# Where the held last product goes at two joins between matmul groups

## Chip, cores and metric

One core of one Trainium2 chip. The metric is the device time of one execution in microseconds (us). The kernel before took 721.73 us (median of 3 runs, 721.68 to 721.85).

## The reference

Layer norm of `x` (2048 tokens of 1024), then two branches on the normed `xn`: a dilated local attention and a gated MLP, joined at the end.

```python
x = A_x
xn = _layernorm(x, axis=-1)
s = _A_ref(xn, A_wqkv, A_wo)                 # qkv = xn @ wqkv; attention over 8 keys, 2 apart; @ wo
g = _silu(_B_ref(xn, B_w1, B_w3, B_w2))      # (silu(xn @ w1) * (xn @ w3)) @ w2
return x + s * g
```

## The kernel before: what the change touches

The q/k/v products and the MLP's first layer run in groups of seven matmul products (a Strassen-like scheme that saves the eighth). A product is eight matmuls of 128x128 weights against 512 columns. A group has three accumulators in PSUM: `pa` ("a" in the profile: aq, am), `pe` ("e") and `pb` ("b"). ScalarE copies a into b, so that b goes on from a's first product.

```python
def seven(key, A, B, e11, e12, e22, e21, snap=None):
    ...
    if snap is None:
        pa = bank2(f"a{key}")
        for i in I:
            mm(pa[:, i], a11[i], b11, True)          # product 1, into a
    pe = bank2(f"e{key}")
    for i in I:
        mm(pe[:, i], s1[i], t1, True)                # product 2, into e
    pb = bank2(f"b{key}")
    act_copy(pb[:], pa[:] if snap is None else snap) # ScalarE: a -> b
    sp5 = k4(f"p{key}")
    act_copy(sp5[:], pe[:])
    if snap is None:
        for i in I:
            mm(pa[:, i], a12[i], b21, False)         # product 3, onto a: has to follow a -> b
        e11(pa)
        flush()                                      # the held product of the group before
    for i in I:
        mm(pb[:, i], s2[i], t2, False)               # product 4, onto b
    su2 = k4(f"u{key}")
    act_copy(su2[:], pb[:])                          # ScalarE: copy of b
    flush()
    ...                                              # products 5 (e12) and 6 (e22: VectorE reads b)
    def tail():
        for i in I:
            mm(pb[:, i], a22[i], t4, False)          # product 7, onto b
        e21(pb)                                      # ScalarE: copies the result out
    pend.append(tail)                                # held for the next group

def qkv_copy(t, c, j0):
    def f(ps, *a):
        ...
            if a:
                ...                                  # VectorE adds
            else:
                nc.scalar.copy(out=d, in_=ps[:])     # e11 and e21 of a q/k/v group
    ...

    qkv_seven(1, 1, wk0, wk1, sk, step)              # k, second half
    flush()                                          # first join
    with behind("v"):
        qkv_sums(wq0, wq1, sk, True)
    qkv_seven(2, 1, *wv, sv, step)                   # v, second half
    qkv_seven(0, 1, wq0, wq1, sk, step)              # q, second half
    flush()                                          # second join, then the MLP
```

So product 7 of a group normally runs after product 3 of the next one. At the two joins `flush()` forced it out at once. (`behind(key)` makes an instruction issue after the one last recorded under that key.)

## Time and profile before

| | before |
|---|---|
| device time, median of 3 | 721.73 us |
| span of the profiled run | 720.1 us |
| PE busy | 712.5 us, 99% |
| granted clock | 0.998 |
| gap between products at the first join | 0.28 us |
| gap at the second join | 0.24 us |

The gaps are not a row of the profile. I measure them from the start times of products in the timeline: the start of a product, less the start of the product before it, less 0.216 us for each of that one's matmuls. The shown end of a matmul won't do, as the prediction explains. The lines of the profile before stand in the prediction.

### The profile page before, as it was taken

To read this page: it belongs to the slowest core of one execution; us is meant where nothing else is said; L and a number is where in the kernel's file an instruction comes from. 1 tells how busy PE (TensorE), PEld (TensorE's weight loads), DVE (VectorE), ACT (ScalarE), POOL (GpSimd) and SP (SyncE) were. 2 spreads that over 40 slices of the span, in tenths; PEclk is the share of its full clock that TensorE was granted. 3 is DMA by queue.
4 is the path that set the end of the run, shared out by engine and by line. 5 is a ranking of instruction groups with operands and counts; after the bars stand their busy time and mean duration, and the time that the engine had idled before them with its cause. 6 is when DMAs were issued, how large, how long until landed. Compare 5 with 4: busy or idle time off the path is not lost.

```text
span 720.1 us, 8820 instructions
## 1 busy us (share of the span) xinstructions
PE 712.5 (99%) x3367; PEld 346.2 (48%) x3367; DVE 625.6 (87%) x697; ACT 314.1 (44%) x329; POOL 95.7 (13%) x162
## 2 busy tenths in 40 slices
PE   8999999999999999999999999999999999999997
PEld 6655565654444444444444444444444444444443
DVE  7996879779879878978999999969859989998975
ACT  5745334356545456555545311024464563120234
POOL 1011100012300000233111000000435004000001
PEclk9999999999999999999999999999999999999999
DMA  9956257867754523457756647469799444463616
GB/s 333 267 146 176 82 185 228 274 228 242 240 174 160 178 85 117 153 205 264 251 169 216 203 132 240 155 189 385 172 279 348 127 152 138 156 205 130 194 55 117
DMA packets 119242, 139.52 MB, mean 194 GB/s; under 512 B 17696, under 2 KB 94496, under 8 KB 118560
## 3 DMA queue, kind: packets, MB, share of 16 engines
q1 hardware_dynamic: 104656, 97.01, 43.3%
q0 software_dynamic: 14544, 41.95, 17.9%
q8 instruction: 26, 0.43, 0.3%
q14 instruction: 16, 0.13, 0.1%
HBM read 96.21 MB, written 38.80 MB: 187 GB/s over the span
## 4 chain that ended last, share of the span: by engine, by line
PE 93%; DVE 2%; ACT 1%; DMA 1%; issue 1%; SPq 0%; DVEq 0%; ACTq 0%
PE bm L151 20%; PE am L151 13%; PE em L151 13%; PE bq L151 9%; PE db L151 8%; PE da L151 7%; PE de L151 6%; PE eq L151 6%; PE aq L151 3%; PE wb L151 3%; PE af L151 2%; PE wa L151 1%; PE we L151 1%; PE af L1038 1%; DMA wring<-in_A_wqkv_dram 1%
## 5 line engine op out<-in xcount | busy, mean ns | idle before, releaser
L151 PEld LDWEIGHTS <-wring 128*128 128x128 f16 (+1 forms) x1792 | 183.4, 103 | 204.2 <-issue 1.6
L151 PEld LDWEIGHTS <-h_sb 128*128 128x128 f16 (+1 forms) x1056 | 109.6, 104 | 118.1 <-issue 0.4
L151 PE MATMUL bm<-xs,wring 128*128 128x512 f16 x504 | 117.4, 379 | 0.1
L151 PE MATMUL am<-xT,wring 128*128 128x512 bf16 x336 | 79.7, 379 | 0.1
L151 PE MATMUL db<-wring,h_sb 128*128 128x512 f16 x336 | 73.2, 379 | 0.0
L481 DVE TENSOR_TENSOR BC<-Ep,vT 128x2048 bf16<-128x2048 bf16 x56 | 66.6, 1216 | 0.1
L426 DVE TENSOR_TENSOR pt<-qt,kT 128x4096 bf16<-128x4096 bf16 x24 | 54.9, 2289 | 0.6
L664 DVE TENSOR_TENSOR um<-em,um 128x1024 f32<-128x1024 f32 x28 | 34.2, 1222 | 21.1 <-PE em L151 20.3
L666 ACT ACTIVATE g<-um 128x1024 bf16<-128x1024 f32 x28 | 29.6, 1057 | 48.6 <-DVE um L664 48.6
L151 PE MATMUL da<-wring,h_sb 128*128 128x512 bf16 x224 | 49.0, 379 | 0.0
L467 POOL DMA_DIRECT2D Ep<-pb x64 | 38.0, 601 | 54.0 <-DVE pb L463 48.3
L151 PE MATMUL bm<-h_sb,wring 128*128 128x512 f16 x168 | 39.7, 379 | 0.0
L151 PE MATMUL em<-xT,wring 128*128 128x512 bf16 x168 | 39.7, 379 | 0.0
L151 PE MATMUL em<-xs,wring 128*128 128x512 f16 x168 | 39.7, 379 | 0.0
L161 ACT COPY bm<-am 128x1024 f32<-128x1024 f32 x28 | 27.9, 998 | 26.0 <-PE am L151 26.0
L491 DVE TENSOR_TENSOR oT<-oT,BC 128x2048 bf16<-128x2048 bf16 x32 | 39.0, 1218 | 0.3
L161 ACT COPY pm<-em 128x1024 f32<-128x1024 f32 x28 | 28.4, 1013 | 20.0 <-PE em L151 20.0
L161 ACT COPY um<-bm 128x1024 f32<-128x1024 f32 x28 | 28.4, 1013 | 18.9 <-PE bm L151 18.9
L685 ACT CAST g<-bm 128x1024 bf16<-128x1024 f32 x28 | 28.3, 1010 | 17.4 <-PE bm L151 17.4
L679 DVE TENSOR_TENSOR h_sb<-bm,pm 128x1024 bf16<-128x1024 f32 x21 | 25.6, 1217 | 5.1 <-PE bm L151 5.0
L428 DVE TENSOR_TENSOR pt<-pt 128x2048 bf16<-128x2048 bf16 x24 | 29.3, 1221 | 0.4
L489 DVE TENSOR_TENSOR BC<-BC 128x2048 bf16<-128x2048 bf16 x24 | 29.3, 1220 | 0.4
(191 smaller groups left out, 996.4 us busy)
## 6 DMA issues: line engine op xcount, KB each, us to landing
wring<-in_B_w_dram SPq DMA_DIRECT2D x61, 512.0 KB, 4.4
wring<-t_dram SPq DMA_DIRECT2D x16, 512.0 KB, 3.9
t_dram<-wring POOLq DMA_DIRECT2D x14, 512.0 KB, 3.9
wring<-t_dram SPq DMA_DIRECT2D x16, 384.0 KB, 5.0
wring<-in_B_w_dram SPq DMA_DIRECT2D x12, 384.0 KB, 4.8
wring<-in_A_x_dram SPq DMA_DIRECT2D x16, 256.0 KB, 4.7
Ep<-pb POOLq DMA_DIRECT2D x64, 64.0 KB, 4.7
wring<-in_A_wo_dram SPq DMA_DIRECT2D x8, 512.0 KB, 5.7
```

The source lines that it names most:

```text
L151: anchor["pe"] = nc.tensor.matmul(ps, lhsT=lhs[k], rhs=rhs[k], start=(first and k == 0), stop=(k == n - 1), skip_group_check=not first,)
L161: nc.scalar.copy(out=out_, in_=in_)
L426: nc.vector.tensor_mul(p_t[:], q[:], kT[:, :, o:o + CH])
L428: nc.vector.tensor_add(p_t[:, 0:4, :], p_t[:, 0:4, :], p_t[:, 4:8, :])
L467: nc.gpsimd.dma_start(out=pr[c][r:P:NR, :, sq * P:(sq + 1) * P], in_=pb[sq * 32:(sq + 1) * 32, :, :])
L481: nc.vector.tensor_mul(dst, E[:, w, :].unsqueeze(1).to_broadcast([P, n, CH]), vT[:, js, o:o + CH])
L489: nc.vector.tensor_add(B, B, C)
L491: nc.vector.tensor_add(A, A, B if w0 else C)
L664: v = nc.vector.tensor_add(su2[:], pe[:], su2[:])
L666: nc.scalar.activation(out=hl["g"][:, :, CH:], in_=su2[:], func=ACTF.Silu)
L679: anchor["v"] = nc.vector.tensor_add(h[:, :, CH:], pb[:], sp5[:])
L685: nc.scalar.copy(out=hl["g"][:, :, 0:CH], in_=pb[:])
```

## The change

Its intent is to let the held product at the two joins wait as it does everywhere else, so that ScalarE makes the new group's copy of a into b first.

```diff
     def act_copy(out_, in_):
         with hp():
-            nc.scalar.copy(out=out_, in_=in_)
+            return nc.scalar.copy(out=out_, in_=in_)
@@ seven
-        act_copy(pb[:], pa[:] if snap is None else snap)
+        anchor["pb"] = act_copy(pb[:], pa[:] if snap is None else snap)
@@ qkv_copy
-                    nc.scalar.copy(out=d, in_=ps[:])
+                    with behind("pb"):
+                        nc.scalar.copy(out=d, in_=ps[:])
@@ the calls
     qkv_seven(1, 1, wk0, wk1, sk, step)
-    flush()
     with behind("v"):
         qkv_sums(wq0, wq1, sk, True)
     qkv_seven(2, 1, *wv, sv, step)
     qkv_seven(0, 1, wq0, wq1, sk, step)
-    flush()
```

## The prediction

> **What bounds the kernel now.** I read the first part of the page first (busy time by engine), then the busy times of five stretches, then the chain of waits near each of the two joins, and last the timeline, instruction by instruction, around the joins and in a later group that the change doesn't touch.
>
> The page's span and busy times:
>
> ```profile
> span 720.1 us, 8820 instructions
> PE 712.5 (99%) x3367; PEld 346.2 (48%) x3367; DVE 625.6 (87%) x697; ACT 314.1 (44%) x329; POOL 95.7 (13%) x162
> ```
>
> The matmul engine (PE) is busy for 99% of the span. The change neither adds nor removes a matmul, so it can gain only what PE loses in gaps. In the view of busy times by stretch the two joins lie in the first and third of these (us of the stretch, its length, then PE):
>
> ```profile
> 102.00:118.00 16.00, 15.88 (x75) 9.48 (x73) 13.82 (x16) 5.95 (x6) 0.53 (x1) 1.00 0.72 237
> 118.00:145.00 27.00, 27.00 (x127) 16.36 (x126) 23.24 (x28) 10.90 (x11) 1.60 (x3) 1.00 0.74 249
> 145.00:172.00 27.00, 26.93 (x131) 13.63 (x129) 22.38 (x32) 17.86 (x19) 1.99 (x3) 1.00 0.79 252
> ```
>
> A stretch without a join shows no idle PE; those with one show 0.12 and 0.07 us. The granted clock is 1.00 in all three. These small figures understate the loss, as the timeline shows. First, what a steady group looks like (timeline, later):
>
> ```profile
> 191.55 1.89 PE L151 MATMUL am<-h_sb,wring 128*128 128x512 bf16 x8
> ...
> 193.28 1.89 PE L151 MATMUL em<-h_sb,wring 128*128 128x512 f16 x8
> ...
> 193.48 1.00 ACT L161 COPY bm<-am 128x1024 f32<-128x1024 f32 x1 [1.07 <-PE am L151]
> ...
> 195.01 1.89 PE L151 MATMUL am<-h_sb,wring 128*128 128x512 bf16 x8
> ```
>
> A product of eight matmuls starts every 1.73 us, 0.216 us per matmul. The third product adds onto the accumulator "a", so it has to follow the copy of "a" into "b" on ScalarE (ACT). That copy starts 0.20 us after the next product has begun (the last "a" matmul still has to land), ends at 194.48, and the third product starts at 195.01 on its own pace: 0.53 us to spare. Now the chain of waits at the first join:
>
> ```profile
> 105.90 1.51 PE aq L151 x7
> 107.41 1.74 PE bq L151 x8
> 109.15 0.03 ACTq L367
> 109.18 0.04 issue
> 109.22 1.01 ACT pk L367
> 110.23 0.92 ACT bq L161
> 111.15 0.04 issue
> 111.20 1.89 PE aq L151 x8
> ```
>
> The chain leaves PE here for two copies on ACT in a row. The last product of the old group (bq at 107.41) ends, its result is copied out (pk, 1.01 us), only then is the new group's "a" copied (bq<-aq), and then PE goes on. The timeline at the second join has the same pattern:
>
> ```profile
> 156.57 1.89 PE L151 MATMUL bq<-h_sb,wring 128*128 128x512 f16 x8
> ...
> 158.30 0.38 PE L151 MATMUL am<-xT,wring 128*128 128x512 bf16 x1
> ...
> 158.50 1.01 ACT L367 CAST h_sb<-bq 128x1024 bf16<-128x1024 f32 x1 [4.09 <-PE bq L151]
> 158.51 1.89 PE L151 MATMUL em<-xs,wring 128*128 128x512 f16 x8
> ...
> 159.41 1.02 ACT L161 COPY bm<-am 128x1024 f32<-128x1024 f32 x1
> ...
> 160.48 1.89 PE L151 MATMUL am<-xT,wring 128*128 128x512 bf16 x8
> ```
>
> **What the Trainium skill says.** (1) Its page "PSUM — Partial Sum Buffer", section "Engine vs sequencer instructions", says that the queues of ScalarE and VectorE are strict FIFO and that matmuls start and complete in program order. The trace agrees: at 158.50 the old group's cast runs, and the new group's copy, whose data were complete by about 158.7 (0.20 us after e began at 158.51), starts at 159.41. (2) The same page, section "PSUM bank collisions raise a hardware error", says that a bank has to be guarded by semaphores against a second engine. That is why the third product waits for the copy of "a" even though it only adds to it; the wait shows as 111.15 to 111.20. (3) "TensorE: Matmul & The Clock Gate", section "Back-to-back issue gap", gives N/2.4 + 2.5 ns, 216 ns at N=512, for one isolated gap, and about 131 ns sustained. The trace has 0.216 us per matmul in a sustained stream, so here the first figure holds and the second doesn't. (4) "Perfetto Trace Analysis", section "Tensor Engine Instruction (MATMUL, LD_WEIGHTS)", says that the profile's end of a matmul is an estimate. The trace bears that out: one matmul is shown as 0.379 us but they start 0.216 us apart, so 0.16 us of every PE gap is covered by the modelled end. I therefore measure gaps from starts.
>
> **The change, part by part.** It removes two calls that force out the held last product at the joins k to v (near 107 us) and q to the MLP (near 157 us). The held product then goes where it goes in all other groups: after the new group's first three products. It also ties the two plain copies of a q/k/v group behind the latest "a" to "b" copy, so that ACT takes that one first. I built the changed program and compared the order of its instructions with that of the kernel before, engine by engine.
>
> PE, first join: before a(7), old tail(8), a(1), e(8), a(8), then b; after a(8), e(8), a(8), old tail(8), then b. Same 32 matmuls, 32 times 0.216 = 6.91 us. Before, the first starts at 105.74 (timeline) and the b product at 112.92: 7.18 us. The stall is thus visible: e starts at 109.19, so the next product could start at 109.19 + 1.73 = 110.92, and it starts at 111.20. That is 0.28 us. (Less the 0.16 that the modelled end covers, it is the 0.12 of the first stretch.)
>
> PE, second join: after a(8), old tail(3), e(8), a(8), old tail(5), then b; the tail is split in two but has the same eight matmuls. Before, e at 158.51 + 1.73 = 160.24 against a start at 160.48: 0.24 us (less 0.16 is the 0.07 of the third stretch).
>
> Is each wait of the new order met in time? Times are on the old clock. First join: a from 105.74, e 107.47, third product 109.19. The copy of "a" starts at 107.47 + 0.20 = 107.67 and takes 1.02: 108.69, so 0.50 us to spare. The tail comes at 110.92 and needs VectorE's read of the same accumulator, which was done at 107.17. The old product's copy then runs from about 112.9 to 113.9, and the next copy that PE needs (of b, before 114.89 in the old trace, 0.28 sooner now) is still free to start on time. Second join: a at 155.06, three tail matmuls at 156.79 (VectorE reads that accumulator 155.26 to 156.48, so 0.3 to spare), e at 157.44, third product at 159.16, with the copy of "a" done by 156.79 + 0.20 + 1.02 = 158.01. Tail at 160.89, b at 161.97 against 162.20 before. ACT then has silu of "a" (1.02 us) from about 161.1, the old cast about 162.2 to 163.2, and the copy of b can start at 163.9: no queue.
>
> VectorE and GpSimd keep their order. On the sync engine's queue two small swaps follow: at the first join the store of v goes ahead of that of k; at the second one 512 KB weight load moves ahead of two copies of x to the output and one spill. That load went out at 165.24 before because it waits for a store; its data are first read by VectorE at 179.14, nearly 14 us later, so this isn't on the path.
>
> Sum: 0.28 + 0.24 = 0.52 us off PE's stream, nothing added on the path. 721.73 - 0.52 = 721.21, some 0.07%.
>
> **Rivals.** First, the gain is given back later. Measured by starts, PE after 20 us has only two more stalls above 0.1 us: 0.28 at 287.45 (ACT: table load, exponential, two copies) and 0.22 at 505.01 (a chain from a weight load through VectorE and ACT). If either were timed by something that doesn't move with PE, it would swallow the gain and the time would stay at 721.7. Against it: both chains start from PE in the view of the chain (the silu of "am" at 282.19; the load issued at 482.97 straight after PE work), so they should slide. VectorE at 87% is the engine that could lag: in 156 to 177 it runs without a break, so the second join's 0.24 isn't passed to it at once. The exponential at 167.01 waits for it, and the next "a" copy at 170.34 queues behind that; PE needs that copy at 172.13 - 0.52 = 171.61, and it would end at about 171.06. Tight, but met; later VectorE idles again (1.25 us at 190.09) and catches up.
>
> Second, the copies collide at the new place: the held product's cast delays the copy of b, and PE waits at the fourth product instead. That would take back up to 0.3 us per join, 721.4 to 721.7. Against it: in all groups without a forced flush this order already runs with no gap.
>
> Third, the moved transfers: three transfers of 512 KB pile up after 165 us rather than at 160, beside loads for the next groups. If one landed over 8 us late, VectorE's sums and then PE would wait, and the time would rise by a microsecond or more. The slack of 14 us against a landing of about 4 us speaks against it.
>
> Fourth, PE's stall at the joins is not really ACT's order, and the gap persists: 721.7. The chain's two adjacent copies with no idle time between speak against it.
>
> **Range and chances.** The three runs before lie within 0.17 us. Full gain is 721.2; half given back 721.5; a slightly better fit of the other stalls and another chip's scatter may reach 720.8. I take 720.8 to 721.65. Two per cent is 14 us; nothing of that size is in reach: faster 0.01, same 0.98, slower 0.01.
>
> **What would show it.** In the profile after, the pieces of ACT should be gone from the chain at 109 to 111 and 158 to 160 us; starts of products should be 1.73 us apart through both joins; busy PE in the first stretch should be 16.00 of 16.00; the copy of "a" should come before the old cast on ACT; the stalls near 287 and 505 should be there still, at 0.2 to 0.3 us, about 0.5 us earlier. The prediction is wrong if a new PE gap stands in the 20 us after either join, if the gaps near 287 or 505 grow by what was gained, or if the weight load of 512 KB holds up VectorE near 179 us.

## The result, and the profile after

The changed kernel took 721.31 us (median of 6 runs, 721.21 to 721.43), beside 721.91 us for the kernel before (6 runs, 721.68 to 722.16). The ratio is 0.9992, with a 95% interval of 0.9979 to 1.0005. A ratio is the mean time of one kernel's fast runs over that of the other's of the same rounds, so not quite the ratio of these medians. The interval reaches past 1, so by itself it doesn't prove a gain of this size. What speaks for it is that every run of the changed kernel was below every run of the kernel before, and the trace.

The page of the changed kernel, its span and busy times:

```profile
span 719.5 us, 8821 instructions
PE 713.1 (99%) x3367; PEld 346.4 (48%) x3367; DVE 625.7 (87%) x697; ACT 314.4 (44%) x329; POOL 96.0 (13%) x162
```

The matmuls are the same 3367. Busy times by stretch (first and third of the stretches shown before; after the stretch and its length stand the busy us of PE, its weight loads PEld, VectorE DVE, ScalarE ACT and GpSimd POOL, then the granted clock and the DMA engines' share and GB/s):

```profile
102.00:118.00 16.00, 16.00 (x76) 9.69 (x75) 13.82 (x17) 6.07 (x6) 0.53 (x1) 1.00 0.70 234
145.00:172.00 27.00, 27.00 (x132) 13.57 (x130) 22.38 (x33) 18.04 (x18) 1.99 (x3) 1.00 0.70 221
```

PE no longer idles in either. The chain of waits (from the end backwards, each step followed to what released it; x8 is eight matmuls) at the first join, changed kernel:

```profile
104.02 1.73 PE bq L151 x8
105.75 1.73 PE aq L151 x8
107.47 1.73 PE eq L151 x8
109.20 1.73 PE aq L151 x8
110.93 3.24 PE bq L151 x15
```

The two ScalarE pieces are gone from it, and products follow at 1.73 us. At the second join, the same view:

```profile
154.79 1.73 PE am L151 x8
156.52 0.65 PE bq L151 x3
157.17 1.78 PE em L151 x8
158.95 1.73 PE am L151 x8
160.67 1.08 PE bq L151 x5
```

The piece of 1.78 us hides a small thing. In the timeline the weight loads (PEld) of that product have a wait of their own:

```profile
156.36 0.81 PE L151 MATMUL bq<-h_sb,wring 128*128 128x512 f16 x3
...
157.04 15.01 PEld L151 LDWEIGHTS <-wring 128*128 128x128 f16 x71 [0.32 <-DVE wring L618]
157.05 1.90 PE L151 MATMUL em<-xs,wring 128*128 128x512 f16 x8
```

Three matmuls from 156.36 end their slots at 157.01, and the next starts at 157.05. Product 2 of the MLP group now comes five matmuls earlier (three of the old product's eight stand ahead of it, where all eight stood), and VectorE has only just made its weights. It costs 0.04 us.

**Where the 0.6 us came from.** Kernels differ a little at the very start, before anything that the change touches. So I take one mark after the start and one at the end: the product on b that starts near 41.8 us, and the last group of matmuls. The span between them, from the timelines of the profiled runs (one run each):

| profiled run | mark | last matmuls start | between | against before | gaps above 0.15 us after the mark |
|---|---|---|---|---|---|
| before | 41.85 | 714.72 | 672.87 | | 0.28, 0.24, 0.28, 0.22 |
| changed | 41.70 | 714.11 | 672.41 | -0.46 | 0.28, 0.22 |
| 1 first join only | 41.87 | 714.46 | 672.59 | -0.28 | 0.23, 0.28, 0.22 |
| 2 second join only | 41.71 | 714.40 | 672.69 | -0.18 | 0.28, 0.28, 0.22 |
| 3 copy order only | 41.68 | 714.04 | 672.36 | -0.51 | 0.28, 0.22 |
| 4 changed again | 41.78 | 714.19 | 672.41 | -0.46 | 0.27, 0.22 |
| 5 flush everywhere | 41.90 | 721.57 | 679.67 | +6.80 | see there |
| 6 the same, copy first | 41.83 | 717.98 | 676.15 | +3.28 | see there |
| 7 third stall | 41.84 | 713.98 | 672.14 | -0.73 | 0.22 |
| 8 four stalls | 41.85 | 715.18 | 673.33 | +0.46 | 0.35, 0.60, 0.45 |
| 9 both orders | 41.72 | 713.80 | 672.08 | -0.79 | 0.23 |
| 10 changed beside 9 | 41.86 | 714.28 | 672.42 | -0.45 | 0.28, 0.22 |

The spans of the profiled runs differ by 0.6 us, 720.1 against 719.5. Of it 0.46 us lies between the marks and 0.15 us before the first, where the mark itself scatters from 41.68 to 41.90 over these profiles. Between the marks: 0.28 + 0.24 gained, 0.04 given to the new wait, makes 0.48; the last 0.02 is within rounding. How well the measure repeats, the three profiles of the changed kernel show: 672.41, 672.41 and 672.42. Of the kernel before there is one profile only. (In the traces of 9 and 10 some matmul records are missing, so there a hole of one matmul after a group shown with seven isn't counted as a gap.)

### The profile page after: what moved, and what is told of

It reads as the page before. It is cut to its first block, busy times and chain, and to the rows that moved or that the text cites. A ratio compares the mean times of both kernels' runs of the same rounds, so it can differ in the third digit from the quotient of the medians.

```text
span 719.5 us, 8821 instructions
## 1 busy us (share of the span) xinstructions
PE 713.1 (99%) x3367; PEld 346.4 (48%) x3367; DVE 625.7 (87%) x697; ACT 314.4 (44%) x329; POOL 96.0 (13%) x162
## 4 chain that ended last, share of the span: by engine, by line
PE 94%; DVE 3%; DMA 1%; ACT 1%; issue 0%; DVEq 0%
PE bm L151 20%; PE am L151 13%; PE em L151 13%; PE bq L151 9%; PE db L151 8%; PE da L151 7%; PE de L151 7%; PE eq L151 6%; PE aq L151 3%; PE wb L151 3%; PE af L151 2%; PE we L151 1%; PE wa L151 1%; DMA wring<-in_A_wo_dram 1%; DVE h_sb L236 1%; PE af L1039 1%
```

## The experiments

The theory: at a join ScalarE's queue holds two copies, the old product's and a into b, in that order; PE needs the second one. The rivals: the time comes from the scatter of the start; the place of the old product among the matmuls is what costs; the gain returns elsewhere as a new wait.

One thing needed no run. I built the changed kernel without the tie (`behind("pb")`), and the kernel before with the tie and both flushes. Compared engine by engine, in instructions and the engines they wait on, the first stands as the changed kernel does and the second as the kernel before. So in this program the tie moves nothing; taking away the two flushes does it all.

Runs 1 to 4 shared one chip and nine runs of the kernel before (median 721.83 us, 721.65 to 722.25).

### 1. The first join alone

```diff
 against the changed kernel
     qkv_seven(0, 1, wq0, wq1, sk, step)
+    flush()
```

> Only the first join (k to v) is changed, the second keeps its forced flush. Theory (the stall at a join is the new group's copy standing behind the old product's copy on ScalarE): no gap between products at the first join, the gap of 0.24 us still there at the second, and 0.28 us less than the kernel before. Rival 1 (the 0.6 us between the medians comes mostly from the start of the kernel, where the first matmuls ran 0.15 us earlier in the profile after): no steady gain, within 0.1 us of before. Rival 2 (the gain needs both joins, because the first only shifts the wait to the second): gap at the second join grows to about 0.5 us, time as before.

Measured: 721.60 us (721.36 to 722.18), ratio 0.9998 (0.9985 to 1.001). The times overlap those of before, so timing alone leaves it open. The trace doesn't: 0.28 us less between the marks. The first join has no gap; at the second the chain still leaves PE:

```profile
158.24 0.23 ACT h_sb L368
...
159.15 1.03 ACT bm L161
160.17 0.04 issue
160.21 1.89 PE am L151 x8
```

The gap there is 0.23 us, not 0.5. So the first join's gain isn't merely moved to the second.

### 2. The second join alone

```diff
 against the changed kernel
     qkv_seven(1, 1, wk0, wk1, sk, step)
+    flush()
     with behind("v"):
```

> Only the second join (q to the MLP) is changed. Theory: the first join keeps its gap of 0.28 us, the second has none of that kind; gain 0.24 us less the 0.04 us for which, in the profile after, the second product of the new group waits for VectorE's weight sums: 0.20 us. Rival (the transfers that swap places on the sync queue matter): an effect of another size than 0.2 us, of either sign, and a gap near 173 to 182 us. Rival 1 (start only): within 0.1 us of before.

Measured: 721.74 us (721.52 to 721.87), ratio 0.9999 (0.9985 to 1.0013); again too small for the timing. The timeline at the second join:

```profile
156.65 0.81 PE L151 MATMUL bq<-h_sb,wring 128*128 128x512 f16 x3
...
157.33 1.19 PEld L151 LDWEIGHTS <-wring 128*128 128x128 f16 x7 [0.33 <-DVE wring L618]
```

In the trace 0.18 us less between the marks, with the 0.04 us wait at 157.34 and no other gap above 0.03 us from there until one of 0.09 us ahead of a small product of the attention scores at 274 us, which all kernels have. So the transfers that swap places (only this join moves the 512 KB load) hold nothing up. The two parts sum to 0.28 + 0.18 = 0.46 us, what the whole change shows.

### 3. Matmuls in the old order, copies in the new

```diff
 against the changed kernel
         def tail():
             for i in I:
                 mm(pb[:, i], a22[i], t4, False)
-            e21(pb)
+            if split[0]:
+                held_out.append(lambda: e21(pb))
+            else:
+                e21(pb)
@@ seven, right after the copy of a into b
+        while held_out:
+            held_out.pop(0)()
@@ at both joins
+    split[0] = True
+    flush()
+    split[0] = False
```

> The forced flushes stay at both joins, so the matmuls run in the order of the kernel before (seven matmuls of a, the old product, the last of a); only ScalarE's order at the two joins is changed: copy of a into b first, then the old product's copy. Theory: that order alone is the cause, so both gaps go and the time is that of the changed kernel, 0.5 us below before. The copy of a should start near 109.4 us, 0.2 us after the last matmul of a, and end near 110.4, 0.5 us ahead of the third product. Rival (it is the place of the old product among the matmuls that costs, for instance its wait for VectorE's read of the same accumulator): both gaps stay, time as before.

Measured: 721.15 us (721.08 to 721.28), ratio 0.9991 (0.9978 to 1.0003); between the marks -0.51 us. The timeline at the first join:

```profile
107.08 1.89 PE L151 MATMUL bq<-h_sb 128*128 128x512 f16 x8
...
109.22 1.00 ACT L161 COPY bq<-aq 128x1024 f32<-128x1024 f32 x1 [5.85 <-PE aq L151]
...
110.13 1.02 ACT L375 CAST pk<-bq 128x1024 bf16<-128x1024 f32 x1
...
110.75 1.89 PE L151 MATMUL aq<-h_sb,wve 128*128 128x512 bf16 x8
```

The old product still stands between the matmuls of a, at 107.08, as before. Only the copies have changed places, and product 3 starts at 110.75, 1.73 us after product 2 at 109.02. Built and compared with the kernel before, engine by engine, this one has the same order on PE, VectorE and GpSimd; two pairs of copies change places on ScalarE, and on the sync engine one store of q goes out behind three other transfers. This settles it for these two joins: ScalarE's order was the cause, the place of the matmuls was not. It even does 0.05 us better than the change in the trace, because product 2 stays where it was and VectorE has its weights ready.

### 4. The changed kernel again

No edit: the changed kernel beside the first three.

> The changed kernel once more, on the same chip and beside the same runs of the kernel before as the first three, so that the parts can be compared with the whole. Theory: 0.45 to 0.6 us below before, equal to the sum of the first two experiments (0.28 + 0.20) within 0.15 us, and equal to the third within 0.15 us.

Measured: 721.28 us (721.16 to 721.35), ratio 0.9992 (0.9979 to 1.0004); -0.46 us between the marks. It agrees with the third within 0.13 us. Its medians don't agree with the sum of the medians of 1 and 2 (0.55 against 0.23 + 0.09) within the 0.15 us that I had set, while the traces agree to 0.01 us: at this size the runs scatter too much to be added up.

Runs 5 to 8 shared another chip and nine runs of the kernel before (median 721.69 us, 721.49 to 722.43).

### 5. A forced flush ahead of every group of the MLP

```diff
 against the kernel before
+            flush()
             seven(f"m{g}_{fb}", up_A(b, fb), ...)
```

> The kernel before, with a forced flush ahead of every group of the MLP as well. ScalarE then has the old product's cast directly ahead of the copy of a into b in 23 more groups. Theory: each of these costs what a join cost, 0.24 to 0.28 us, so 23 times 0.26 = 6.0 us: 727.9 us, and 23 new gaps of that size between products. Rival (a gap at a join is peculiar to the q/k/v stage, or is taken up by slack elsewhere): under 2 us. Rival (the old product also waits for VectorE, which is busier in the MLP): more than 8 us, with gaps ahead of the old product rather than ahead of the third product.

Measured: 728.57 us (728.40 to 729.34), ratio 1.0097 (1.0081 to 1.0112). This is the effect enlarged until the timing shows it without doubt. The chain of waits of one such group:

```profile
195.47 1.01 ACT g L685
196.48 0.92 ACT bm L161
197.41 0.04 issue
197.45 1.67 PE am L151 x7
```

There are 22 new gaps of 0.23 to 0.24 us ahead of product 3, 5.1 us together. That is one fewer and a little smaller than foreseen. The rest of the 6.8 us is some 1.7 us net. Of it 1.5 us stand ahead of the old product, 0.04 to 0.05 us after the end of VectorE's read of the same accumulator (0.4 us at 169.34, 0.49 at 305.57 and a row of 0.03 to 0.12): the second rival is right about nearly a quarter of the loss. Another 0.33 us ahead of the old product is not VectorE but a load of its weights:

```profile
563.61 1.89 PE L151 MATMUL bm<-xs,wring 128*128 128x512 f16 x8 [0.17 <-DMA wring<-s_dram]
```

The stall near 504 us grows by 0.11 us (at 510.37 here), and that near 287 us (0.28) is gone.

### 6. The same flushes, a into b first

```diff
 against the fifth experiment (with the lines of the third for held_out and split)
+            split[0] = True
             flush()
+            split[0] = False
@@ e21 of an MLP group (called after the copy of a into b)
-                    nc.scalar.copy(out=hl["g"][:, :, 0:CH], in_=pb[:])
+                    with behind("pb"):
+                        nc.scalar.copy(out=hl["g"][:, :, 0:CH], in_=pb[:])
```

> As the one before, with the old product forced out ahead of the new group's second product in every MLP group, but its cast placed behind the copy of a into b on ScalarE (26 groups). The two joins of the q/k/v stage are as in the kernel before. Theory: no loss, 721.9 within 0.5 us, and the third product of each group starts on its own pace. Rival (the matmuls' order costs, not ScalarE's): the same loss as in the run before, about 6 us.

Measured: 725.05 us (724.82 to 725.09), ratio 1.0045 (1.0033 to 1.0058). My expectation of no loss failed: 3.4 us are lost. All 22 gaps ahead of product 3 in the MLP groups are gone. So the theory holds for those, and 5 and 6 differ by 3.5 us. But 6 is not 5 with ScalarE's order alone changed. The timelines show that in two groups PE also takes product 6 earlier, by four matmuls (at 289.67 us) and by five (at 595.02), and two of the gaps of 6 stand just there. What I had left out is that the old product, forced forward, follows closely on VectorE's read of the same accumulator. Its largest gap, in the chain of waits (e22 on VectorE, then the old product):

```profile
303.39 1.22 DVE wring L686
304.61 0.04 issue
304.65 1.89 PE bm L151 x8
```

This gap is 0.73 us, where the fifth run had 0.49: PE, freed from ScalarE, comes to VectorE earlier and waits there instead. That it waits there because it is freed is my reading. With 0.41 at 169.28, 0.34 at 328.95 and 0.24 at 598.71 that makes 1.7 us on VectorE. A load at 560 us (0.57), a longer stall of product 6 near 290 us (0.56 against 0.28; a table load and an activation stand ahead of the copy of b), 0.23 at 595.02 (again an activation ahead of the copy of b) and small ones make up the rest. These shares are read from the chain alone; no run separates them. At the two joins VectorE's read was done in time, which is why experiment 3 loses nothing.

### 7. The stall near 287 us

The same pattern stands there: product 6 of a group needs ScalarE's copy of b, which stood behind the cast of the old product (and an exponential with its table load). In the changed kernel:

```profile
284.83 1.89 PE L151 MATMUL em<-xT,wring 128*128 128x512 bf16 x8
284.88 0.99 ACT L686 CAST g<-bm 128x1024 bf16<-128x1024 f32 x1
285.77 1.02 ACT L161 COPY um<-bm 128x1024 f32<-128x1024 f32 x1
...
286.84 1.89 PE L151 MATMUL bm<-xs,wring 128*128 128x512 f16 x8
```

```diff
 against the changed kernel
+            if key == "m1_4":
+                held_out.append(lambda: e21(pb))
+            else:
                 e21(pb)
@@ seven
-        act_copy(su2[:], pb[:])
+        anchor["su"] = act_copy(su2[:], pb[:])
+        while held_out:
+            held_out.pop(0)()
         flush()
@@ e21 of that group: its cast with behind("su")
```

> The changed kernel, and at the stall near 287 us the cast of the old product (one group alone) behind ScalarE's copy of b, which the fourth product after it waits for. Theory (the same mechanism: a copy that the matmuls need stands behind one that they don't): the gap of 0.28 us goes, 0.28 us below the changed kernel, about 0.8 us below before. Rival (the exponential and the table load ahead of both are the bound, not the cast): gap stays or only shrinks by less than half.

Measured: 721.01 us (720.76 to 721.10), ratio 0.9989 (0.9977 to 1.0002); -0.73 us between the marks, 0.27 below the changed kernel. The same stretch of its timeline:

```profile
284.98 1.89 PE L151 MATMUL em<-xT,wring 128*128 128x512 bf16 x8
285.23 1.01 ACT L161 COPY um<-bm 128x1024 f32<-128x1024 f32 x1
286.14 1.02 ACT L693 CAST g<-bm 128x1024 bf16<-128x1024 f32 x1
286.70 1.89 PE L151 MATMUL bm<-xs,wring 128*128 128x512 f16 x8
```

The copy runs ahead of the cast, and the product at 286.70 comes 1.72 us after the one before: no gap. The exponential and the table load stayed ahead of both, so they alone weren't the bound.

### 8. The stall near 504 us as well

```diff
 against the seventh experiment
@@ exponents, for the third chunk only: the exponential is put off until
@@ the output projection has emitted its copy of b, and the work that
@@ needs it waits for that
-        with fore():
-            nc.scalar.activation(out=z, in_=z, func=ACTF.Exp, scale=scale)
+        def exp():
+            with fore(), behind("su") if c == 2 else nullcontext():
+                nc.scalar.activation(out=z, in_=z, func=ACTF.Exp, scale=scale)
+        wait_su.append(exp) if c == 2 else exp()
```

> As the run before, and at the stall near 504 us the exponential is placed behind the copy of b on ScalarE; this also moves some attention work on VectorE by one group. Theory: the fourth gap of 0.22 us goes too, about 1.0 us below before, if VectorE's new order makes no wait of its own. Rival: VectorE's order changes enough to put a new gap in front of a later product, and the gain is lost.

Measured: 722.04 us (721.90 to 722.29), ratio 1.0004 (0.9992 to 1.0017); +0.46 us between the marks. The fourth gap is gone, but three new ones stand at 558.81, 571.50 and 604.33 (0.35, 0.60 and 0.45 us). One of them in the chain:

```profile
555.54 1.23 DVE um L679
556.77 0.02 issue
556.79 1.06 ACT g L681
557.85 0.92 ACT bm L161
558.77 0.04 issue
558.81 1.24 PE am L151 x5
```

The rival is right that the gain is lost; the sum fits: -0.73 - 0.22 + 1.40 = +0.45. My reading, not shown, is that putting the exponential off also put off VectorE's work on the attention weights, and that its backlog comes out where VectorE is busiest. The edit changes more than that: PE's order too is another one (the eight small matmuls of the score sums run at 590.58 us, in the seventh run at 577.75; two products near 504 us change places). So the run shows that the whole edit loses, not which of these moves does it.

### 9 and 10. Three gaps by ScalarE's order alone

```diff
 against the seventh experiment
@@ both joins (the old product's copy put off as in the third experiment)
+    split[0] = True
+    flush()
+    split[0] = False
```

The ninth puts 3 and 7 together; the tenth, without an edit, is the changed kernel beside it (eleven runs of before, median 721.87 us, 721.63 to 722.63).

> The flushes stay at both joins with only ScalarE's order changed there (as in the third experiment), and the one cast near 287 us goes behind the copy of b (as in the seventh). Theory: the three gaps of 0.28, 0.24 and 0.28 us are gone and no wait of 0.04 us for VectorE's weight sums is added: 0.80 us below the kernel before, 0.3 us below the changed kernel beside it. Rival (the effects don't add up, for instance because a gap taken out early comes back where VectorE or a transfer sets the pace): less than 0.6 us below before, with a new or longer gap after 287 us.

> The changed kernel beside the ninth experiment, on the same chip: 0.45 to 0.6 us below before, 0.2 to 0.4 us above the ninth.

Measured: the ninth 721.15 us (720.91 to 721.64), ratio 0.9989 (0.9977 to 1.0001); the tenth 721.42 us (721.05 to 723.96), ratio 0.9998 (0.9986 to 1.001), where one run of 723.96 us pulls the mean. Between the marks -0.79 and -0.45 us, so the effects add up to 0.01 us (0.51 + 0.27 = 0.78) and the ninth is 0.34 us below the changed kernel in the trace. It has no gap at 287 us and no wait at 157 us. It is the best version that I have; by runs alone it is not separated from the changed kernel.

## Why the prediction was right

- *What bounds the kernel.* Right. PE stayed at 99%, and only its gaps moved.
- *The cause of the gaps.* Right. Experiment 3 tests it more narrowly than the change itself does: it leaves the matmuls where they were and has the whole gain.
- *The sizes, 0.28 and 0.24 us.* Right: each join alone shows 0.28 and 0.18 + 0.04 us. The sum of 0.52 was a little high, since the trace shows 0.46.
- *"Is each wait of the new order met in time?"* Here one step was missing. I checked ScalarE's copies and VectorE's reads, but not the weights of product 2 at the second join, which VectorE makes just then; moving it forward by five matmuls made it wait 0.04 us. The trace of the kernel before could have told me: there VectorE ends these weights at 157.41 us (156.73 + 0.68), and the prediction has the product start at 157.44. In the changed kernel it starts 0.06 us after the end of this work (156.99 to 157.05), so 157.44 was too early by 0.03 us. So "nothing added on the path" was not quite true.
- *A reason that doesn't carry.* Under (2) the prediction explains product 3's wait for the copy of a by the rule that two engines must not use one bank at once. The kernel needs that wait in any case: product 3 adds onto a, and b has to start from a's first product alone. No run here shows the bank rule at work. And 111.15 to 111.20 us is the hand-over after the copy; the wait that costs is 110.92 to 111.20. The sums don't rest on this reason.
- *Rival 1, given back later.* Refuted. The stalls near 287 and 504 us slid along at 0.28 and 0.22 us.
- *Rival 2, copies colliding at the new place.* Refuted: no gap ahead of product 4.
- *Rival 3, transfers.* Refuted: the load went out at 163.25 us instead of 165.24, and no gap follows.
- *Rival 4, another cause.* Refuted by 3 and 5.
- *The time.* 721.21 was predicted from 721.73. The measured 0.6 us between medians is more than the 0.46 us of the trace. I can't say what the other 0.14 us is; the scatter of the start is of that size. That the measured 721.31 comes so near is in part luck: the kernel before stood at 721.91 in six runs, 0.18 us above the 721.73 from which I had subtracted.

## What to carry to other kernels

On an engine that takes its queue in order, look for a copy that another engine waits for standing behind a copy that nobody waits for, and swap these two before moving anything on the engine that is the bound. Measure such gaps from start to start, and enlarge a doubtful effect (here 22 times) when it is smaller than the scatter of the runs, and read in the trace which other waits grew with it. Taking away one wait brings PE sooner to the next one: check every operand of what moves forward, weights included.

## What the Trainium skill lacked or had wrong

- "TensorE: Matmul & The Clock Gate", section "Back-to-back issue gap": it gives about 131 ns per matmul for a sustained stream at N=512, below its isolated figure of 216 ns. In this sustained stream, at a granted clock of 1.00, it is 0.216 us (1.73 us for eight) in every trace here. It is this section that is wrong: elsewhere the same page has back-to-back matmuls at a spacing that agrees with these traces.
- "Perfetto Trace Analysis", section "Tensor Engine Instruction (MATMUL, LD_WEIGHTS)": it says that the end is estimated, but not how much idle time that hides. Here each gap loses 0.16 us (0.379 shown, 0.216 from start to start): gaps of 0.28 and 0.24 us show as 0.12 and 0.07 us of idle PE. Both terms can be worked out from formulas on the page "TensorE: Matmul & The Clock Gate", but neither page draws the difference.
- No page was found to have a figure for the hand-over between PE and ScalarE, on which the slack of such a group rests. Here the copy starts 0.20 us after the next product has begun (193.28 to 193.48), and PE starts 0.04 to 0.05 us after a copy's shown end (111.15 to 111.20).
